# Chunks 0 to 3 of w_in: the low part from an fp32 product by the identity, and a new written order of the first phase

## The chip, the cores and the metric

One Trainium2 chip; the program runs on one of its cores. The time is device microseconds of one execution. The engines are TensorE (PE; PEld is its weight load), VectorE (DVE), ScalarE (ACT), GpSimd (POOL) and SyncE (SP), which issues nearly all DMAs here. Each engine takes its instructions strictly in the order in which the program gives them, and waits where an operand or a buffer is not ready.

## What is computed

Three layers in a row, for 4 batches of 576 tokens (heads of 64, model width 512):

```python
attn = softmax(q @ k.T / 8 - slope*|i-j|, over 128 keys back) @ v     # 8 heads, fp32
h = relu(x @ w_in); u, v = h[..., :512], h[..., 512:]                  # w_in: 512 x 1024
v_n = (v - mean(v)) / sqrt(var(v) + 1e-6)
gated = u * (w_spatial @ v_n + b_spatial)                              # 576 x 576
x = gated @ w_out                                                      # 512 x 512
out = sum over the best 2 of 4 experts of gate * (causal attention with wq, wk, wv) @ wo
```

w_in and w_out come as 64-bit floats, the rest as 32-bit floats. Products that need more than one pass are made from two parts of each factor, high and low, each rounded for TensorE's one-pass fp32 type (fp32r): high times high, high times low, low times high.

## The kernel before

The **first phase** covers the first attention and the spatial layer up to `gated`; the **second phase** folds w_out into the expert weights (`pw`, the product that opens it), projects (`pq`, `pvB`) and runs the causal attention. This change edits the first phase and a few lines at the start of the second.

In the first phase everything is cut into small steps with names, and three strings hold the order in which they are written: `OPENING`, `FIRST` and `SECOND` (lines 38 to 113). `step` (a nested function) turns a name into instructions. Within `OPENING` the order on every engine but the weights' own loads is exactly that of the string: an engine's program is the sequence of its own steps, so two steps that stand side by side but belong to different engines do not order one another. In `FIRST`, `SECOND` and the second phase only TensorE's order is written and a scheduler sets the others.

The steps that matter below. Tiles are numbered 0 to 19 in the order of the attention (batch 0: blocks 0, 1, 2, 3, 4 of 128 queries, the last of 64; batch 1 on: block 4 first).

- `raw n`, `q n`, `k n`, `v n`, `W n.ld`, `O n.ld`: loads on SP's queue. `raw` is a 128 x 512 chunk of w_in in 64-bit words; there are 8 chunks, 0 to 3 for the half of w_in that makes v, 4 to 7 for the half that makes u. Four buffers hold raw chunks and three hold q blocks, so a later load waits until an earlier chunk or block has been read.
- `C n.x`: chunk n is turned from 64-bit words into a high and a low part (lines 305 to 331). `abs` (ACT), `shl`, `or`, `mask`, `mul` (DVE, lines 379 to 382) give an fp32 value `w` and a remainder; `high` (ACT, line 320) rounds w; `rest` (DVE, line 207, called `lo_part`) subtracts the rounded value from w; `add` and `sec` (PE, lines 327 and 329) sum `rest` and the remainder in PSUM by products with an fp32r identity `one`; `low` (ACT, line 331) rounds the sum.
- `s i.g` (PE, lines 462 and 465): the scores of tile i for half g of the heads, fp32. `l i.g.*` (DVE, lines 480 and 229): mask and row minimum. `e i.g.*` (ACT, line 230): exponential and row sum. `f i.g.*` (DVE, lines 487 to 489): division by the sum. `t i.g` (PE, line 502): transposes. `c i.g` (ACT, line 504): eviction. `g i.g.*` (POOL): triangles. `a i` (PE, line 529): product with v. `xh i`, `xl i` (ACT line 541, DVE line 207): high and low part of the attention's output, which is the x of the next layer.
- `V b.t.n` (PE, line 555): a third of the product x times the v-half of w_in, for 128 tokens. `U b.s.m.n` (PE, line 618): a third of the u-half's. `P b.m.s.n` (PE, lines 633 and 636): a third of the spatial product; `pm` (DVE), `gs` (SP) gate and store it.
- `+n` behind a name: n fills, transposes of the identity into a PSUM bank that the step then overwrites (line 337). `warm` (line 344) issues 15 of them at the very start. They compute nothing.

One PSUM tile holds either a transposed tile or an attention product (`psT`, one buffer), two hold scores (`psS`), three hold the products of C, V, U and P (`psD`). So `t` and `a` follow each other through one buffer, with an eviction between any two.

At the start of the second phase, after the eight tiles of `pw`, `proj` of batch 0 runs while `gparts`, the copies of batch 1's gated values into `x2`, are spread between its parts.

Of the kernel before, what the change touches and what calls it, by code (L numbers as in the profile page):

```python
# [42 lines left out]
    t0.0 f1.0.rec C3.shl c0.0 l1.1.0 l1.1.1 l1.1.2 e1.1.0 a0 l1.1.3 e1.1.2 C3.or e1.1.1 q3 f1.0.mul s2.0 C3.high q4 C3.mask e1.1.3 l2.1.cp xh0 q5
    f1.1.add C3.rest l2.1.0 C3.add+8 l2.1.1 e2.1.0 l2.1.2 l2.1.3 e2.1.1 xl0 e2.1.2 f1.1.rec e2.1.3 C3.mul t1.0 f2.1.add C2.mul c1.0 C3.sec C3.low
    l2.0.cp g1.0.0 C2.sec raw6 C4.abs s3.0 f2.1.rec raw7 f1.1.mul C2.low W0.ld f2.1.mul C5.abs W1.ld t1.1 l2.0.0 g1.0.1 l2.0.1 V0.0.0 e2.0.0 l2.0.2
    l2.0.3 c1.1 C5.shl C4.shl e2.0.2 s3.1 C5.or e2.0.1 e2.0.3 C4.or t2.1 C5.high q6 f2.0.add g1.1.0 l3.0.cp C4.high V0.0.1 c2.1 f2.0.rec g1.1.1
    l3.1.cp V0.0.2 g2.1.0 W0.hi l3.0.0 l3.0.1 l3.0.2 e3.0.0 a1 g2.1.1 l3.0.3 l3.1.0 r0.0 l3.1.1 f2.0.mul W1.hi bn0.0 e3.1.1 e3.0.2 C4.mask s4.0 v7 xh1
    ag0.0 C5.mask C4.rest e3.1.0 e3.0.1 xl1 C4.add+4 e3.0.3 C5.mul t2.0 V0.1.0 f3.0.add C4.mul c2.0 l4.0.cp C6.abs g2.0.0 C4.sec f3.0.rec l3.1.2
    V0.1.1 l4.0.0 C4.low l4.0.1 g2.0.1 l3.1.3 e4.0.0 s4.1 C6.shl e4.0.1 f3.0.mul C7.abs a2 k10 f4.0.add e3.1.2 C6.or e3.1.3 q7 f4.0.rec C7.shl C6.high
    f3.1.add C6.mask s5.1 f3.1.rec f4.0.mul xh2 v8 f3.1.mul V0.1.2 xl2 C6.mul t3.1 r0.1 V0.2.0 C6.rest c3.1 bn0.1 g3.1.0 t3.0 C6.add ag0.1 C7.or c3.0  # L50
    C6.sec V0.2.1 C6.low l4.1.cp g3.1.1 l5.1.cp C7.high l4.1.0 g3.0.0 V0.2.2 l4.1.1 e4.1.0 l5.1.0 l5.1.1 g3.0.1 e4.1.1 t4.0 e5.1.0 s5.0 f4.1.add
    C7.mask c4.0 f4.1.rec e5.1.1 C5.rest a3 r0.2 q8 l5.0.cp g4.0.0 f5.1.add l5.0.0 g4.0.1 l5.0.1 e5.0.0 bn0.2 e5.0.1 s6.0 C7.rest xh3 v10 s6.1 ag0.2
    C7.mul n0.2.ln C7.add n0.2.ex q9 xl3 C7.sec C5.add O0.ld C7.low C5.sec f4.1.mul V0.3.0 f5.0.add O1.ld n0.2.r0 C5.low f5.1.rec f5.0.rec n0.2.r1
    f5.1.mul f5.0.mul t4.1 U0.1.1.0 W1.lo c4.1 U0.1.1.1 l6.0.0 g4.1.0 l6.0.1 t5.0 e6.0.0 l6.0.2 g4.1.1 U0.1.1.2 l6.0.3 e6.0.1 n0.2.r2 W0.lo U0.1.0.0
    c5.0 ur0.1.1 n0.2.r3 g5.0.0 a4 e6.0.3 W2.ld N0.0.sc O0.abs W3.ld N0.1.sc N0.0.hi s7.0 N0.2.sc v11 N0.1.hi N0.0.lo xh4 U0.1.0.1 N0.1.lo N0.2.hi
    V0.3.1 xl4 g5.0.1 e6.0.2 W2.hi N0.2.lo V0.3.2 W3.hi f6.0.add W2.lo t5.1 r0.3 U0.1.0.2 W3.lo W4.ld c5.1 U0.0.2.0 f6.0.rec ur0.1.0 bn0.3 W5.ld
    g5.1.0 U0.0.2.1 l6.1.0 g5.1.1 ag0.3 l6.1.1 U0.0.2.2 e6.1.0 l6.1.2 l6.1.3 e6.1.1 U0.0.3.0 l7.0.cp ur0.0.2 U0.0.0.0 e6.1.3 f6.0.mul e6.1.2 U0.0.0.1
    l7.0.0 W4.hi l7.0.1 t6.0 f6.1.add l7.0.2 e7.0.0 f6.1.rec U0.0.0.2 l7.0.3 W4.lo c6.0 U0.0.1.0 ur0.0.0 f6.1.mul U0.0.1.1 W5.hi O0.shl U0.0.1.2 O0.or
    t6.1 e7.0.1 U0.0.3.1 ur0.0.1 W5.lo c6.1 U0.0.3.2 O0.mask e7.0.2 a5 O0.mul e7.0.3 ur0.0.3 f7.0.add O0.add O2.ld s7.1 xh5 f7.0.rec f7.0.mul O0.hi
    s8.0 xl5 q10 O0.sh O0.lo a6 l7.1.cp O0.sl U0.1.2.0 l8.0.cp xh6 V0.4.0 l7.1.0 xl6 e7.1.0 l8.0.0 V0.4.1 l8.0.1 e8.0.0 l8.0.2 l8.0.3 e8.0.1 l7.1.1  # L60
    t7.0 l7.1.2 e8.0.2 l7.1.3 V1.0.0 e8.0.3 c7.0 f8.0.add f8.0.rec V1.0.1 e7.1.2 f8.0.mul e7.1.1 g7.0.0 e7.1.3 V1.0.2 O1.abs f7.1.add g7.0.1 f7.1.rec
    U0.1.2.1 r1.0 f7.1.mul U0.1.2.2 O1.shl t7.1 bn1.0 ur0.1.2 V0.4.2 c7.1 O1.or ag1.0 g7.1.0 t8.0 r0.4 U0.1.3.0 O1.mask c8.0 bn0.4 g7.1.1 U0.1.3.1
    U0.1.3.2 g8.0.0 ag0.4 n0.4.ln a7 O1.mul n0.4.ex ur0.1.3 n0.4.r0 g8.0.1 O3.ld n0.4.r1 n0.4.r2 n0.4.r3 O1.add s8.1 N0.3.sc xh7 v12 N0.4.sc N0.3.hi
    s9.1 xl7 q11 N0.4.hi l8.1.cp V1.1.0 N0.3.lo l8.1.0 V1.1.1 l8.1.1 l8.1.2 e8.1.0 l8.1.3 l9.1.cp e8.1.1 s9.0 e8.1.3 N0.4.lo e8.1.2 O1.hi V1.1.2 q12
    f8.1.add l9.1.0 O1.sh l9.1.1 e9.1.0 O1.lo P0.0.0.0 k15 e9.1.1 P0.0.0.1 l9.0.cp r1.1 O1.sl P0.0.0.2 l9.1.2 l9.0.0 e9.1.2 l9.1.3 l9.0.1 U1.0.0.0
    e9.0.0 l9.0.2 l9.0.3 e9.0.1 U1.0.0.1 pm0.0.0 e9.1.3 f8.1.rec bn1.1 U1.0.0.2 e9.0.3 P0.0.1.0 e9.0.2 f8.1.mul ur1.0.0 P0.0.1.1 f9.0.add f9.1.add
    ag1.1 f9.0.rec f9.1.rec t8.1 f9.0.mul P0.0.1.2 f9.1.mul c8.1 P0.1.0.0 g8.1.0 pm0.0.1 t9.1 gs0.0 g8.1.1 O2.abs P0.1.0.1 c9.1 P0.1.0.2 O2.shl O2.or
    U1.0.1.0 pm0.1.0 g9.1.0 U1.0.1.1 O2.mask U1.0.1.2 g9.1.1 a8 ur1.0.1 O2.mul O2.add O2.hi s10.1 v13 xh8 s10.0 O2.lo v14 P0.1.1.0 xl8 O2.sh q13
    l10.1.0 P0.1.1.1 l10.0.0 e10.1.0 l10.0.1 O2.sl P0.1.1.2 l10.0.2 e10.0.0 l10.0.3 l10.1.1 e10.0.2 l10.1.2 P0.2.0.0 l10.1.3 e10.0.1 pm0.1.1 P0.2.0.1
    e10.1.2 gs0.1 e10.0.3 P0.2.0.2 e10.1.3 f10.0.add e10.1.1 f10.0.rec U1.0.2.0 f10.0.mul P0.2.1.0 pm0.2.0 O3.abs P0.2.1.1 f10.1.add f10.1.rec  # L70
    f10.1.mul U1.0.2.1 O3.shl U1.0.2.2 O3.or P0.2.1.2 ur1.0.2 O3.mask P0.3.0.0 pm0.2.1 P0.3.0.1 O3.mul gs0.2 P0.3.0.2 O3.add U1.0.3.0 O3.hi pm0.3.0
    U1.0.3.1 O3.lo O3.sh U1.0.3.2 P0.3.1.0 O3.sl ur1.0.3 P0.3.1.1 P0.3.1.2 V1.2.0 pm0.3.1 gs0.3 t9.0 V1.2.1 c9.0 g9.0.0 t10.0 V1.2.2 c10.0 g9.0.1
    t10.1 r1.2 s11.1 c10.1 bn1.2 a9 ag1.2 l11.1.cp n1.2.ln n1.2.ex l11.1.0 n1.2.r0 l11.1.1 e11.1.0 l11.1.2 l11.1.3 e11.1.1 s11.0 n1.2.r1 v15 xh9
    n1.2.r2 n1.2.r3 N1.2.sc v16 e11.1.3 s12.0 xl9 e11.1.2 q14 N1.2.hi l11.0.cp a10 f11.1.add l12.0.cp U1.1.0.0 f11.1.rec xh10 l11.0.0 f11.1.mul
    U1.1.0.1 e11.0.0 l11.0.1 U1.1.1.0 l11.0.2 e11.0.1 l12.0.0 l11.0.3 U1.1.0.2 e11.0.2 l12.0.1 l12.0.2 e12.0.0 U1.1.2.0 l12.0.3 xl10 e12.0.2 U1.1.2.1
    e12.0.1 N1.2.lo U1.1.2.2 e12.0.3 ur1.1.0 N1.0.sc U1.1.1.1 e11.0.3 f12.0.add N1.1.sc U1.1.1.2 ur1.1.2 N1.0.hi f11.0.add f12.0.rec U1.1.3.0
    f11.0.rec f12.0.mul ur1.1.1 U1.1.3.1 N1.1.hi f11.0.mul U1.1.3.2 N1.0.lo t11.0 ur1.1.3 N1.1.lo V2.0.0 c11.0 g11.0.0 t11.1 V2.0.1 c11.1 g11.0.1
    g11.1.0 V2.0.2 g11.1.1 V1.3.0 r2.0 bn2.0 V1.3.1 ag2.0 V1.3.2 t12.0 r1.3 s12.1 c12.0 bn1.3 g12.0.0 a11 ag1.3 l12.1.cp q15 n1.3.ln g12.0.1 n1.3.ex
    l12.1.0 n1.3.r0 l12.1.1 e12.1.0 n1.3.r1 l12.1.2 e12.1.1 n1.3.r2 s13.1 l12.1.3 v17 n1.3.r3 xh11 N1.3.sc e12.1.2 xl11 s13.0 e12.1.3 N1.3.hi l13.1.cp
    V2.1.0 l13.0.cp q16 l13.1.0 l13.0.0 V2.1.1 e13.1.0 l13.0.1 l13.0.2 e13.0.0 l13.0.3 l13.1.1 e13.0.2 V2.1.2 l13.1.2 l13.1.3 e13.0.3 f12.1.add  # L80
    N1.3.lo e13.1.2 s14.0 r2.1 f12.1.rec f12.1.mul e13.1.3 s14.1 e13.1.1 bn2.1 t12.1 e13.0.1 q17 f13.1.add ag2.1 f13.1.rec P1.0.0.0 f13.0.add
    f13.1.mul c12.1 P1.0.0.1 l14.1.cp g12.1.0 f13.0.rec P1.0.0.2 l14.1.0 l14.1.1 e14.1.0 g12.1.1 P1.0.1.0 e14.1.1 pm1.0.0 P1.0.1.1 f13.0.mul t13.1
# [1119 lines left out]
```

## Time and profile before

| | us |
|---|---|
| median of 3 runs | 478.71 (478.48 to 478.85) |
| the profiled execution | 478.61 |
| its span in the trace | 476.9 |
| PE busy | 464.6 (97%) |
| PEld busy | 412.4 (86%) |
| DVE busy | 303.6 (64%) |
| ACT busy | 266.2 (56%) |

The span runs from the first instruction to the last; 1.7 us of the execution's time lie outside it. Busy shares are means over the whole span: the opening looks quite different from the rest. PE's records overlap by a part of their length, so PE's busy time overstates what it costs to run a row of matmuls; where the chain of work that ended last passes through PE, its pieces show the spacing instead. [...]

### The profile page before, as it was taken

To read this page: it belongs to the slowest core of one execution; us is meant where nothing else is said; L and a number is where in the kernel's file an instruction comes from. 1 tells how busy PE (TensorE), PEld (TensorE's weight loads), DVE (VectorE), ACT (ScalarE), POOL (GpSimd) and SP (SyncE) were. 2 spreads that over 40 slices of the span, in tenths; PEclk is the share of its full clock that TensorE was granted. 3 is DMA by queue.
4 is the path that set the end of the run, shared out by engine and by line. 5 is a ranking of instruction groups with operands and counts; after the bars stand their busy time and mean duration, and the time that the engine had idled before them with its cause. 6 is when DMAs were issued, how large, how long until landed. Compare 5 with 4: busy or idle time off the path is not lost.

```text
span 476.9 us, 10486 instructions
## 1 busy us (share of the span) xinstructions
PE 464.6 (97%) x3867; PEld 412.4 (86%) x3867; DVE 303.6 (64%) x1100; ACT 266.2 (56%) x793; POOL 94.2 (20%) x208
## 2 busy tenths in 40 slices
...
GB/s 259 377 263 93 182 168 180 89 191 150 96 52 67 92 52 49 0 1 26 51 290 107 160 60 100 1 101 0 2 23 3 1 45 1 1 1 68 90 89 88
DMA packets 22518, 43.75 MB, mean 92 GB/s; under 512 B 3522, under 2 KB 5954, under 8 KB 22084
## 3 DMA queue, kind: packets, MB, share of 16 engines
...
## 4 chain that ended last, share of the span: by engine, by line
PE 94%; DVE 3%; DMA 2%; ACT 1%; issue 0%; POOL 0%; POOLq 0%; ACTq 0%; DVEq 0%
PE pu L618 11%; PE pv L555 11%; PE pg L633 11%; PE pq L909 10%; PE px L529 7%; PE pvB L871 6%; PE pxB L1025 6%; PE ps L462 5%; PE pout L1060 5%; PE ptB L1004 5%; PE psB L958 4%; PE pw L774 4%; PE pt L502 3%; PE pg L636 2%; DMA q<-in_qP 2%; PE psB L960 1%
## 5 line engine op out<-in xcount | busy, mean ns | idle before, releaser
L230 ACT ACTIVATE p<-p,st 128x128 f32<-128x128 f32 x144 | 56.4, 394 | 11.6 <-DVE st L229 11.2
L909 PE MATMUL pq<-x,W 128*128 128x288 f32 x384 | 58.5, 302 | 0.8 <-DVE k L207 0.8
L555 PE MATMUL pv<-win,x 128*128 128x512 f32 x216 | 57.8, 407 | 0.0
L633 PE MATMUL pg<-wsp,vn 128*128 128x288 f32 x384 | 57.7, 297 | 0.0
L511 POOL TENSOR_SCALAR_AFFINE_SELECT pU<-pT 128x512 f32<-128x512 f32 (+1 forms) x32 | 20.0, 624 | 183.9 <-ACT pT L504 181.7
L618 PE MATMUL pu<-x,win 128*128 128x288 f32 x384 | 56.1, 298 | 0.0
L909 PEld LDWEIGHTS pq<-x,W 128*128 128x128 f32 x384 | 52.0, 188 | 3.7 <-issue 1.7
L633 PEld LDWEIGHTS pg<-wsp,vn 128*128 128x128 f32 x384 | 52.9, 188 | 0.6 <-issue 0.2
L618 PEld LDWEIGHTS pu<-x,win 128*128 128x128 f32 x384 | 52.2, 188 | 1.1 <-issue 0.7
L242 POOL TENSOR_SCALAR pB<-pB,stB 128x384 f32<-128x384 f32 (+4 forms) x64 | 35.7, 575 | 69.6 <-DVE stB L981 58.3
L555 PEld LDWEIGHTS pv<-win,x 128*128 128x128 f32 x216 | 39.1, 191 | 8.6 <-issue 1.0
L230 ACT ACTIVATE pB<-pB,stB 128x128 f32<-128x128 f32 (+3 forms) x64 | 35.6, 558 | 14.7 <-DVE stB L229 14.7
L504 ACT COPY pT<-pt 128x512 f32<-128x512 f32 (+1 forms) x40 | 21.6, 540 | 29.1 <-PE pt L502 28.9
L462 PE MATMUL ps<-k,q 64*128 64x256 f32 (+1 forms) x256 | 31.2, 378 | 3.1 <-DMA q<-in_qP 2.0
L229 DVE CUSTOM_DVE_ANT_0 pB<-psB,trit 128x128 f32<-128x128 f32 (+3 forms) x64 | 28.2, 486 | 9.2 <-PE psB L958 8.9
L229 DVE CUSTOM_DVE_ANT_0 p<-ps,relm 128x128 f32<-128x128 f32 x128 | 29.7, 282 | 4.1 <-PE pt L502 2.5
L1004 PE MATMUL ptB<-ident,pB 128*128 128x128 f32 (+1 forms) x200 | 30.3, 274 | 0.3 <-DVE pTB L1005 0.3
L641 DVE TENSOR_TENSOR g<-u,pg 128x288 f32<-128x288 f32 x32 | 14.3, 452 | 24.8 <-PE pg L636 23.2
L462 PEld LDWEIGHTS ps<-k,q 64*128 64x128 f32 x256 | 21.8, 193 | 9.2 <-issue 3.2
L1060 PE MATMUL pout<-wo,o 128*128 128x512 f32 x102 | 29.6, 412 | 0.0
L1025 PE MATMUL pxB<-pTB,vt 128*64 128x128 f32 (+2 forms) x480 | 28.3, 262 | 0.0
L1025 PEld LDWEIGHTS pxB<-pTB,vt 128*64 128x64 f32 (+1 forms) x480 | 23.1, 136 | 5.6 <-issue 3.4
...
## 6 DMA issues: line engine op xcount, KB each, us to landing
...
gf<-g_dram SPq DMA_DIRECT2D x4, 1152.0 KB, 5.6
raw<-in_w_in SPq DMA_DIRECT2D x8, 512.0 KB, 6.9
...
k<-in_kP SPq DMA_DIRECT2D x3, 1152.0 KB, 7.0
rawo<-in_w_outT SPq DMA_DIRECT2D x4, 512.0 KB, 5.1
```

What stands on the lines that cost most here:

```text
L229: lambda: nc.vector.tensor_tensor_reduce(s_view, ps_view, tab, -0.125, FLT_MAX, ALU.add, ALU.min, nm),
L230: lambda: nc.scalar.activation(s_view, s_view, AF.Exp, bias=nm, scale=-1.0, accum_out=sm),
L242: nc.gpsimd.tensor_scalar(p, p, r, 0.0, op0=ALU.mult, op1=ALU.add)
L462: nc.tensor.matmul(ps[:, o, 256 * h : 256 * h + kn], Q_[b, j][r, hp, :], K_[b][r, hp, k0 : k0 + kn], start=True, stop=True)
L529: nc.tensor.matmul(px[64 * o : 64 * o + 64, hp, :qn], V_[b, t][:, h * 64 : h * 64 + 64], rhs, start=(t == max(0, j - 1)), stop=(t == j))
L555: nc.tensor.matmul(pv, x[i][:, k, t0 : t0 + P], win[j][:, k, 512:1024], start=(n == 0 and k == 0), stop=(n == 2 and k == 3))
L618: nc.tensor.matmul(pu[:, :HALF], win[i][:, k, m * P : (m + 1) * P], x[j][:, k, c], start=(n == 0 and k == 0), stop=(n == 2 and k == 3))
L633: nc.tensor.matmul(pg[:, :HALF], vn[i][k][:, m * P : (m + 1) * P], wsp[j][:, k, c], start=(n == 0 and k == 0), stop=False)
L909: nc.tensor.matmul(pq[:, :HALF], W[i][:, k, c0 : c0 + P], G[j][:, k, c], start=(n == 0), stop=(n == 11))
L1004: nc.tensor.transpose(pt[:kb, n, :], p[pr][:, o, c0 : c0 + kb], ident)
L1025: nc.tensor.matmul(px[64 * o : 64 * o + 64, pr, :qn], vt[:kb, c, (2 * pr + o) * 64 : (2 * pr + o) * 64 + 64], rhs, start=(c == 0), stop=(c ...
L1060: nc.tensor.matmul(po[:tn], o2[i][:, pr, :tn], wos[j][:, pr, :], start=(n == 0), stop=(n == 5))
```

## The change

For chunks 0 to 3 of w_in the step `rest` is gone. TensorE takes w itself in full fp32 by the fp32 identity (`sum`), subtracts the rounded value by a second fp32r product with minus the identity (`minus`), and adds the remainder as before (`sec`). Chunks 4 to 7 keep `rest`, `add` and `sec`. One ACT instruction at the start makes the negative identity. The three strings are new: the same steps otherwise, in another order on every engine and on SP's queue; of the 50 fills (23, 15, 8 and 4) 6 are left, ahead of the first scores. The first strip of the second phase issues the copies into `x2` ahead of `proj` instead of between its parts.

```diff
 OPENING = """
-    raw0 q0 k0 raw1 raw2 k2 k1 q1 T1 T0 C0.abs q2 C0.shl C0.or C0.mask C0.high v0 C0.mul C0.rest C0.add+23 C0.sec k3 s0.1 C0.low s0.0 l0.1.0 l0.1.1
...
+    T1 raw0 q0 k0 raw1 C0.abs q1 k1 s0.1+6 s0.0 k2 raw2 q2 raw3 q3 C0.shl C0.or C0.mask C0.mul C0.high T0 l0.1.0 l0.1.1 l0.1.2 l0.1.3 C0.sum C0.minus
...
     one = const.tile([P, P], F32R, name="one")
+    minus = const.tile([P, P], F32R, name="minus")
     nc.scalar.copy(one, ident)
+    nc.scalar.mul(minus, ident, -1.0)
...
-        elif name == "add":
+        elif name in ("add", "sum"):
             live[n].append(psD.tile([P, 512], F32, tag="D", name=f"psw{n}"))
-            fill(live[n][4][:, :P])
-            nc.tensor.matmul(live[n][4], one, live[n][3], start=True, stop=False)
+            fill(live[n][-1][:, :P])
+            first = (ident, live[n][1]) if name == "sum" else (one, live[n][3])
+            nc.tensor.matmul(live[n][-1], *first, start=True, stop=False)
+        elif name == "minus":
+            nc.tensor.matmul(live[n][-1], minus, hi, start=False, stop=False)
         elif name == "sec":
-            nc.tensor.matmul(live[n][4], one, lo, start=False, stop=True)
+            nc.tensor.matmul(live[n][-1], one, lo, start=False, stop=True)
...
     G, gparts = load_g(1, gfp)
-    dense.pull(3000.0)
     for _ in gparts:
-        dense.pull(1500.0)
+        pass
     dense.drain()
```

SP's queue, loads 4 to 15 of the program before (`raw` a chunk of w_in, `q`, `k`, `v` blocks of the attention's inputs; the trailing number is a buffer's):

```order
L298 DMA raw_184<-in_w_in 128x512
L298 DMA raw_186<-in_w_in 128x512
L437 DMA k_182<-in_kP 128x4x128 x2
L432 DMA q_1_190<-in_qP 128x512
L432 DMA q_2_194<-in_qP 128x512
L445 DMA v_0_200<-in_v 128x512
L437 DMA k_182<-in_kP 128x4x128
L298 DMA raw_248<-in_w_in 128x512
L298 DMA raw_261<-in_w_in 128x512
L660 DMA reltail<-in_relt 128x512
L437 DMA k_182<-in_kP 128x4x64
L439 DMA k_295<-in_kP 128x2304
```

The block q 3 stands only 9 loads behind this piece, after 3 loads of v, raw 5 and 4 more of v. The same place now:

```order
L300 DMA raw_186<-in_w_in 128x512
L437 DMA q_1_190<-in_qP 128x512
L442 DMA k_184<-in_kP 128x4x128 x2
L300 DMA raw_210<-in_w_in 128x512
L437 DMA q_2_212<-in_qP 128x512
L300 DMA raw_214<-in_w_in 128x512
L437 DMA q_3_216<-in_qP 128x512
L450 DMA v_0_281<-in_v 128x512
L450 DMA v_1_283<-in_v 128x512
L300 DMA raw_285<-in_w_in 128x512
L437 DMA q_4_287<-in_qP 128x512
L442 DMA k_184<-in_kP 128x4x128
```

q 3 has moved to the tenth place of the queue, and the whole K of batch 1 (128x2304) from the fifteenth to the twenty-fifth.

PE, the last rows before the first product with w_in (`pv`, step V 0.0.0) in the program before (`ps` scores, `pt` transposes, `psw` the sums of the chunks):

```order
L462 MATMUL ps_2_0_394<-k_182,q_2_194 128x256 x4
L337 MATMUL psw_413<-ident 128x128 x8
L327 MATMUL psw_413<-vn_3_115,one 128x512
L502 MATMUL pt_1_0_433<-ident,p_1_0_312 128x128 x4
L329 MATMUL psw_413<-win_99,one 128x512
L329 MATMUL psw_357<-win_99,one 128x512
L462 MATMUL ps_3_0_454<-k_182,q_3_391 128x256 x4
L502 MATMUL pt_1_1_475<-ident,p_1_1_362 128x128 x4
L555 MATMUL pv_0_485<-win_98,x_102 128x512 x4
```

And now:

```order
L330 MATMUL psw_367<-u_108,ident 128x512
L332 MATMUL psw_367<-win_100,minus 128x512
L467 MATMUL ps_3_1_370<-k_184,q_3_216 128x256 x4
L334 MATMUL psw_367<-win_101,one 128x512
L330 MATMUL psw_376<-u_109,ident 128x512
L507 MATMUL pt_1_0_393<-ident,p_1_0_263 128x128 x4
L332 MATMUL psw_376<-win_100,minus 128x512
L334 MATMUL psw_376<-win_101,one 128x512
L507 MATMUL pt_1_1_404<-ident,p_1_1_315 128x128 x4
L560 MATMUL pv_0_411<-win_100,x_104 128x512 x4
```

The fills are gone, each chunk has three products instead of two, and the scores of tile 3 that need q 3 stand some way ahead of the first `pv` instead of just before it.

## Rows read from the trace of the kernel before

**Rows 1.** Stretches: us; busy (instructions) of PE, PEld, DVE, ACT, POOL; clock; DMA share; GB/s
```profile
5.76:32.11 26.35, 20.04 (x138) 14.49 (x137) 24.76 (x92) 17.85 (x59) 3.55 (x6) 0.92 1.05 350
32.11:35.50 3.39, 3.39 (x15) 2.10 (x13) 0.98 (x4) 2.78 (x9) 1.27 (x2) 0.61 0.33 128
5.76:76.85 71.09, 64.53 (x526) 52.25 (x524) 65.56 (x236) 54.95 (x171) 14.95 (x25) 0.95 0.68 223
110.00:271.90 161.90, 161.90 (x1321) 148.29 (x1320) 98.17 (x341) 78.40 (x248) 21.39 (x40) 1.00 0.25 85
```
**Rows 2.** Timeline of PE: start, us, instruction, [idle before, releaser]
```profile
29.34 2.08 PE L462 MATMUL ps<-k,q 64*128 64x256 f32 x8 [2.04 <-DMA q<-in_qP]
32.11 2.05 PE L555 MATMUL pv<-win,x 128*128 128x512 f32 x4
76.98 0.77 PE L529 MATMUL px<-pT,v 128*64 128x128 f32 x10
271.92 1.39 PE L774 MATMUL pw<-wc,wt 128*128 128x386 f32 x7
294.62 1.58 PE L909 MATMUL pq<-x,W 128*128 128x288 f32 x10 [0.76 <-DVE k L207]
```
**Rows 3.** Chain of work that ended last, pieces on PE: start, us of the piece
```profile
49.76 0.46 PE pt L502 x4
50.22 0.23 PE psw L327
50.45 0.23 PE psw L329
52.74 0.65 PE ps L465 x4
53.46 1.97 PE px L529 x32
55.43 1.09 PE ps L462 x16
57.65 0.93 PE pv L555 x4
58.79 1.06 PE pu L618 x8
61.14 1.08 PE px L529 x32
62.22 1.06 PE ps L462 x8
```
**Rows 4.** Groups of instructions on DVE, 0 to 110 us: shapes, count, busy us, mean ns
```profile
L229 DVE CUSTOM_DVE_ANT_0 p<-ps,relm 128x128 f32<-128x128 f32 x68 | 15.7, 280 | 1.5 <-PE ps L462 1.5
...
L207 DVE TENSOR_TENSOR vn<-u,win 128x512 fp32r<-128x512 f32 x8 | 5.4, 679 | 0.0
...
L207 DVE TENSOR_TENSOR wsp<-st_wsp,wsp 128x576 fp32r<-128x576 f32 x4 | 2.9, 745 | 0.0
```
**Rows 5.** Timeline of DVE: the first chunk's first step, and the low part of tile 5
```profile
5.76 0.43 DVE L379 TENSOR_SCALAR u<-f 128x512 int32<-128x512 int32 x1 [2.02 <-ACT f L378]
10.19 0.29 DVE L229 CUSTOM_DVE_ANT_0 p<-ps,relm 128x128 f32<-128x128 f32 x1 [1.48 <-PE ps L462]
76.17 0.68 DVE L207 TENSOR_TENSOR x<-px,x 128x512 fp32r<-128x512 f32 x1
```
**Rows 6.** DMA issues by line: count, KB each, median us from issue to landing
```profile
raw<-in_w_in SPq DMA_DIRECT2D x8, 512.0 KB, 6.9
k<-in_kP SPq DMA_DIRECT2D x3, 1152.0 KB, 7.0
```
**Rows 7.** Timeline of PE in the first 9 us: warm-up transposes and fills
```profile
1.42 3.46 PE L344 MATMUL warm<-ident 128*128 128x128 f32 x15 [1.42 <-POOL ident masks.py:199]
6.81 1.37 PE L337 MATMUL psw<-ident 128*128 128x128 f32 x8
```
**Rows 8.** Busy time by stretch around the wait for q 3
```profile
28.00:30.00 2.00, 0.66 (x4) 0.57 (x6) 2.00 (x11) 1.33 (x4) 1.79 (x4) 0.50 1.05 398
```

More of the change, by code (lines that the diff above doesn't have):

```diff
@@ L43 @@
[L43 to L82, printed above, removed]
@@ new lines @@
+    C0.sec s1.0 l0.0.0 l0.0.1 l0.0.2 e0.1.0 C1.abs e0.1.3 e0.1.2 e0.1.1 C1.shl l0.0.3 C1.or f0.1.add C1.mask s1.1 e0.0.0 e0.0.1 f0.1.rec C1.mul
+    l1.0.cp f0.1.mul l1.0.0 l1.0.1 l1.0.2 l1.0.3 C0.low e0.0.2 e0.0.3 C2.abs C1.high f0.0.add e1.0.1 C3.abs v0 v1 raw4 q4 k3 reltail v2 k4 raw5 C1.sum
+    t0.1 C1.minus s2.1 C1.sec c0.1 e1.0.0 e1.0.2 e1.0.3 l1.1.cp C2.shl l1.1.0 f0.0.rec l1.1.1 f0.0.mul l1.1.2 l1.1.3 t0.0 s2.0 C2.or l2.1.cp C3.shl
+    l2.1.0 l2.1.1 f1.0.add C2.mask l2.1.2 l2.1.3 C3.or C2.mul f1.0.rec C3.mask e1.1.0 c0.0 C1.low e1.1.3 e1.1.1 C2.high e1.1.2 a0 C2.sum C2.minus s3.1
@@ new lines @@
+    C2.sec C3.sum e2.1.3 e2.1.2 xh0 C4.abs C3.high f1.1.add f1.0.mul xl0 f1.1.rec C3.mul f1.1.mul e2.1.0 e2.1.1 C2.low t1.0 c1.0 C3.minus C3.sec
+    C3.low t1.1 V0.0.0 V0.0.1 V0.0.2 C5.abs c1.1 g1.0.0 g1.0.1 g1.1.0 g1.1.1 l2.0.cp f2.1.add l2.0.0 l2.0.1 l2.0.2 l2.0.3 f2.1.rec C5.shl e2.0.3
+    e2.0.2 e2.0.1 e2.0.0 f2.1.mul l3.1.cp t2.1 l3.1.0 f2.0.add l3.1.1 f2.0.rec l3.1.2 f2.0.mul l3.1.3 s3.0 r0.0 c2.1 t2.0 c2.0 e3.1.3 e3.1.2 s4.1
+    g2.1.0 g2.1.1 g2.0.0 g2.0.1 a1 C5.or l3.0.cp l3.0.0 l4.1.cp l3.0.1 e3.1.1 e3.1.0 l3.0.2 l3.0.3 e3.0.3 xh1 e3.0.0 e3.0.1 l4.1.0 l4.1.1 C4.shl C4.or
@@ new lines @@
+    xl1 e3.0.2 f3.1.add f3.1.rec f3.1.mul C5.mask f3.0.add C5.mul C4.mask C4.mul f3.0.rec C5.high raw6 v3 v4 raw7 W0.ld k5 e4.1.0 e4.1.1 s4.0 q5 q6
+    W1.ld W1.hi q7 s5.0 a2 xh2 W0.hi V0.1.0 V0.1.1 V0.1.2 C6.abs C7.abs C4.high xl2 f4.1.add f4.1.rec C5.rest f4.1.mul C6.shl C7.shl f3.0.mul t3.1
+    C5.add C5.sec c3.1 V0.2.0 t3.0 V0.2.1 V0.2.2 g3.1.0 g3.1.1 l4.0.cp C7.or l4.0.0 l4.0.1 c3.0 g3.0.0 g3.0.1 C7.mask C6.or l5.0.cp t4.1 C7.high r0.1
+    C5.low c4.1 s5.1 l5.0.0 l5.0.1 C4.rest l5.1.cp C6.mask l5.1.0 C7.mul l5.1.1 C7.rest e5.0.0 a3 s6.1 s6.0 C4.add C7.add C7.sec C4.sec e5.0.1 xh3
@@ new lines @@
+    r0.2 xl3 e4.0.0 e4.0.1 C6.high e5.1.0 C6.mul f4.0.add f5.0.add f4.0.rec f4.0.mul f5.0.rec C6.rest C4.low V0.3.0 t4.0 V0.3.1 C6.add C6.sec V0.3.2
+    C7.low c4.0 e5.1.1 C6.low bn0.1 f5.0.mul W0.lo W1.lo l6.0.0 l6.0.1 l6.0.2 t5.0 l6.1.0 l6.1.1 l6.0.3 bn0.2 l6.1.2 r0.3 e6.0.2 c5.0 bn0.0 f5.1.add
+    O0.ld q8 q9 O1.ld W2.ld W3.ld U0.1.0.0 U0.1.0.1 U0.1.1.0 U0.1.1.1 U0.1.1.2 U0.1.0.2 O0.abs e6.0.1 e6.0.0 e6.1.0 ur0.1.1 e6.0.3 g4.0.0 g4.1.0
+    g4.1.1 g5.0.0 g5.0.1 g4.0.1 U0.1.3.0 a4 xh4 e6.1.2 e6.1.1 ur0.1.0 l6.1.3 e6.1.3 f5.1.rec O0.shl O0.or O0.mask f6.0.add O0.mul f5.1.mul xl4
```

86 lines of the change are left out of this document (55 added, 31 removed).

## The prediction

> **What bounds the kernel now.** I read the time by stretch first. From 110 to 271.9 us PE is busy for all of 161.9 us at the full clock [rows 1]; after that its timeline shows one gap, 0.76 us before a `pq` at 294.62 [rows 2]. So from about 35 us on nothing but PE's own work counts, and the time is that work plus what PE lost before. The opening is another stage: between 5.76 and 32.11 us DVE is busy for 24.76 of 26.35 us, PE for 20.04, and the DMA engines are full (share 1.05, 350 GB/s) [rows 1]. DVE, which turns w_in into two parts, all but sets the opening, and the loads come next.
>
> The timeline of PE then shows where q 3 landed: its scores start at 29.34 after an idle 2.04 us, the first `pv` (V 0.0.0) not before 32.11 [rows 2]. [...]
>
> To put a number on the loss I use the **lateness** of a step: its start, less all PE work written ahead of it. The prices are pieces of the chain of waits, where records don't overlap [rows 3]: four transposes or fills 0.46, so 0.11 each; a product of 512 columns in the one-pass type 0.23; a third of V 0.93, of U 0.53; a half's scores 1.06 (0.55 in the first block, 0.65 in the last); an attention product 1.97 (1.08 for 64 queries). Ahead of V 0.0.0 stand 16.1 us of work: it is 16.0 late. Ahead of tile 5's two-part product with v (the piece of ten that starts near 76.98 [rows 2] is its neighbour, and holds the start, about 77.06) stand 58.4 us: 11.2 V, 9.5 U, 14.2 scores, 5.3 transposes, 9.0 attention, 3.7 for the 16 products that split w_in, 5.5 for 50 fills. It is 18.7 late. At the fold (271.92 [rows 2], 252.2 of work ahead) it is 19.7. All that this change can gain is in these 19 us, or in the work itself.
>
> **The change, part by part.**
>
> *Work on PE.* 44 fills go: 44 x 0.11 = -4.84. `minus` takes the place of `add` at the same 0.23: nothing. Four `sum` are added, fp32 with 512 columns. No such product is in the trace; the nearest is the scores of the last block, 0.65 for four records that are two products of 192 columns [rows 3], so 1.69 ns a column and 0.87 for 512. [...] I take 0.87, the row of the real product: +3.48. Sum -1.4.
>
> *Work on DVE.* Four `rest` go, 0.68 each [rows 4]: -2.7. The new order also carries steps over this place. I compare up to the same step, the low part of tile 5 (76.17, done 76.85 [rows 5]). Behind it go three low parts of v_n, one row statistic and two low parts of the spatial weights (0.68 and 0.75 a piece [rows 4]) with three small ones: -4.7. Ahead of it come half a softmax (four row pieces of 0.28 [rows 4] with their readouts, a mask, two small ones) and five passes over a chunk of w_out: +5.5. The 65.6 us of DVE work in 5.76 to 76.85 [rows 1] become 63.7.
>
> *Loads.* Ahead of q 3 stood 8064 KB, now 3584. It landed at 29.34; by its share of the bytes it lands near 13 to 14, long before its scores are written. The 2.04 us hole goes, and with it DVE's idle 2.4 us behind it (3.39 less 0.98 [rows 1]). What is late next in the opening is the first softmax: DVE sat 1.48 us ahead of 10.19 until the scores came [rows 5]; I leave that in.
>
> *The opening, then.* DVE starts at 5.76 on the first chunk [rows 5]. Up to the low part of chunk 3 the new order has 18.1 us of its work; with 1.5 idle and 0.44 for eviction, V 0.0.0 starts near 25.8, with 15.2 us of PE work ahead: 10.6 late instead of 16.0. PE could not catch up by more, as its products follow DVE's parts.
>
> *The attention of batch 0.* With 63.7 us of DVE work and the old idle 5.5 (71.09 less 65.56 [rows 1]) less the hole's 2.4, the low part of that tile is done at 5.76 + 63.7 + 3.1 = 72.6. PE has 61.3 us ahead of the product behind it (six U thirds and one half's scores more than before, four sums, six fills): 11.3 late, 7.4 less than before. From there on PE was never kept waiting before, and in the new order no producer stands nearer to its consumer on PE.
>
> *The fold and the drain.* ACT's four copies into `x2` stand right behind the same eviction in both orders, and PE's order there is unchanged. I cost this at nothing: behind it lies the pull of the weight products, and the 0.76 us gap at 294.62 [rows 2] stays, some 9 us earlier. If that cover fails, the same gap grows by at most one eviction of four, under 2 us. The negative identity, 0.3 us of ACT while it waits for the first load, is hidden.
>
> **Sum:** -1.4 of work and -7.4 of lateness, -8.8. Against the profiled execution's 478.61 (span 476.9) that is 469.8; the median of the runs shown is 478.71, 0.1 above it, so **469.9**.
>
> *Bounds.* With no idle DVE the lateness is 10.2 for V 0.0.0's chain: 468.7. Sums at 0.44 take 1.7 more: 467.0. With all the old idle of 5.5 on DVE the lateness is 13.7: 472.2. [...]
>
> [...] The fills are what kept PE busy. [...] The gap of 2.04 us was followed by 0.50 [rows 8]. [...]
>
> **The rivals.**
>
> 1. *The clock stays low in the opening (slower).* After the warm-up transposes end at 4.9 us PE has only six fills and then scores that wait for q 0, k 0 and the first chunk; nothing fills the waits for DVE. In its place: everything up to V 0.0.0. [...] 478.6 - 1.4 + 3.7 = **480.9**. It decides from a lateness of 20.1, that is 8.7 us lost to the clock, some 17 us at the lower level on the path. For it: 0.50 after a gap of only 2.04 us [rows 8]. Against it: DVE is the slower engine in this stage, so PE at half speed has slack to lose first; and PE's 15 us of work in 20 are not far from its old share.
>
> 2. *A late load takes the place of q 3.* The new queue puts the K of batch 1 (1152 KB, 7.0 us from issue to landing [rows 6]) ahead of the v block that tile 5's product in the new order needs, and the queue stands behind a load that waits for DVE's low part of a w_out chunk: 53.4 us of DVE work, near 62.1. The K goes out then, the v block lands near 69.5, and PE arrives at 58.1 + 11.3 = 69.4. There is no margin: 2 to 3 us lost once would give **472.5**. For: eight chunks of 512 KB took 6.9 us each to land in a full queue [rows 6]. Against: at 60 us the queue is no longer full (0.68 over the whole stretch against 1.05 in the opening [rows 1]).
>
> 3. *Only the work counts.* The lateness is made again somewhere in FIRST by DVE, whose 65.56 of 71.09 us [rows 1] leave it little slack, and only the 1.4 of work and one or two us stay: about **476**. For: DVE loses only 1.9 us of work up to the place compared. Against: the hole of 2.04 us and the idle of DVE behind it are gone for a reason that the queue shows.
>
> 4. *The change does nothing for the time.* It would need the lateness to come out at 20, rival 1 at half strength: within 1 us of 478.7.
>
> **How the numbers follow.** The forecast with its bounds (467.0 to 474.5, rival 2 within it) has 0.78, rival 3 (474.5 to 477.7) 0.09, rival 4 0.03, rival 1 0.10. About 0.2%, 1 us, is what a measurement of this kernel can tell from no change. So faster 0.87, same 0.03, slower 0.10. The range 467.0 to 474.5 leaves out rivals 1, 3 and 4, 0.22 together, so I stretch it to 475.0, which takes in a little of rival 3.
>
> **What the profile of the changed kernel would show.** Right: the scores of tile 3 start without a wait for q 3, which lands before 15 us; V 0.0.0 starts at 25 to 27; DVE has no gap over 1.5 us from 8 to 35 us; `sum` rows of 0.87 us; the first `pw` near 263; the 0.76 us gap near 286. Wrong: a granted clock near 0.5 over most of 7 to 25 us, with V 0.0.0 past 30 (rival 1); PE idle near 70 us, released by a load of v (rival 2); V 0.0.0 on time but the fold at 270 (rival 3). If `sum` takes over 1.2 us the product is not what I priced; if the `pq` gap grows, the drain is not free.

## The result, and the profile after

The changed kernel takes 474.15 us (median of 4 runs, 473.99 to 474.43) against 478.6 us beside it: ratio 0.991, 95% interval 0.9893 to 0.9927. It is faster by 4.5 us, about half of the 8.8 that the prediction gave. The time lies inside the range; the forecast itself was almost twice too large.

PE's timeline of the changed kernel, at the places of [rows 2] and at the longest of its waits from there on (start us, us, engine, line, operation, tiles; in brackets the idle time before and what ended it):

```profile
24.07 3.01 PE L560 MATMUL pv<-win,x 128*128 128x512 f32 x12
...
29.51 0.63 PE L507 MATMUL pt<-ident,p 128*128 128x128 f32 x4 [0.52 <-DVE p L494]
...
35.27 0.44 PE L534 MATMUL px<-pU,v 128*64 128x128 f32 x4 [0.90 <-DVE st L492]
...
71.08 0.34 PE L534 MATMUL px<-pU,v 128*64 128x64 f32 x4 [0.96 <-DMA v<-in_v]
...
74.47 0.66 PE L507 MATMUL pt<-ident,p 128*128 128x128 f32 x4 [0.16 <-DVE x L209]
...
245.56 6.67 PE L623 MATMUL pu<-x,win 128*128 128x288 f32 x48 [1.03 <-ACT u L626]
...
266.94 17.19 PE L779 MATMUL pw<-wc,wt 128*128 128x386 f32 x96
285.30 12.94 PE L914 MATMUL pq<-x,W 128*128 128x288 f32 x96 [1.17 <-DVE W L209]
```

The wait for q 3 is gone, and V 0.0.0 starts at 24.07 instead of 32.11. The fold, the clearest mark of what the first phase cost, starts 4.98 us earlier than in [rows 2]. The rest of the program got 0.5 us longer, nearly all of it in the wait ahead of the first `pq`. Behind 40 us three waits are new: 0.96 us for a load of v, 1.03 us for an eviction of u, and 1.17 us where 0.76 stood before.

Busy time by stretch, to set beside [rows 1] (us; busy us and instructions of PE, PEld, DVE, ACT, POOL; clock; DMA share; GB/s):

```profile
5.76:24.07 18.31, 16.34 (x106) 10.10 (x105) 18.21 (x74) 16.17 (x57) 0.33 (x1) 1.00 1.01 338
24.07:37.16 13.09, 11.35 (x107) 9.06 (x105) 12.81 (x49) 10.08 (x37) 8.27 (x12) 1.00 0.72 253
28.00:30.00 2.00, 1.48 (x13) 1.06 (x14) 2.00 (x12) 0.58 (x1) 1.27 (x2) 1.00 1.03 424
```

VectorE is busy for 18.21 of the 18.31 us up to V 0.0.0: it all but sets that stage. The granted clock, given as a share of its full speed, reads 1.00 in all three stretches, with six fills; the 0.50 of [rows 8] is gone. (The trace's record of the clock begins at 7.08 us here and at 7.48 before; the 1.00 ahead of that is a blank, not a reading.)

The lateness of the prediction (a step's start less the PE work ahead of it, by the same prices) shows where the gain went (us):

| step | before | after | gained in lateness |
|---|---|---|---|
| V 0.0.0 | 32.11 - 16.1 = 16.0 | 24.07 - 15.2 = 8.9 | 7.1 |
| behind tile 5's product | 18.5 to 18.7 | 74.47 - 61.3 = 13.2 | 5.4 |
| u product at 245.56 (after) | 19.7 | 14.8, then 16.1 behind its wait | 4.9, then 3.6 |
| fold | 271.92 - 252.2 = 19.7 | 266.94 - 250.8 = 16.1 | 3.6 |

The 3.6 and the 1.4 of work saved are the 5.0 at the fold.

### The profile page after: what moved, and what is told of

The parts are those of the page before. It is cut to its first block, busy times and chain, and to the rows that moved or that the text cites. A ratio compares the mean times of both kernels' runs of the same rounds, so it can differ in the third digit from the quotient of the medians.

```text
span 472.4 us, 10405 instructions
## 1 busy us (share of the span) xinstructions
PE 460.4 (97%) x3831; PEld 407.7 (86%) x3831; DVE 302.2 (64%) x1096; ACT 263.5 (56%) x794; POOL 97.0 (21%) x208
## 4 chain that ended last, share of the span: by engine, by line
PE 85%; DMA 4%; ACT 3%; DVE 3%; SPq 2%; issue 1%; ACTq 0%; DVEq 0%
PE pq L914 11%; PE pg L638 10%; PE pv L560 9%; PE pu L623 8%; PE px L534 6%; PE pvB L876 6%; PE pxB L1030 6%; PE pout L1065 5%; PE ptB L1009 5%; PE psB L963 4%; PE ps L467 4%; PE pw L779 4%; PE pt L507 3%; DMA raw<-in_w_in 2%; PE pg L641 2%; DMA st_wsp<-in_wspT 2%
## 5 line engine op out<-in xcount | busy, mean ns | idle before, releaser
L638 PE MATMUL pg<-wsp,vn 128*128 128x288 f32 x384 | 58.7, 297 | 0.0
L516 POOL TENSOR_SCALAR_AFFINE_SELECT pU<-pT 128x512 f32<-128x512 f32 (+1 forms) x32 | 21.8, 688 | 167.4 <-ACT pT L509 167.1
L560 PE MATMUL pv<-win,x 128*128 128x512 f32 x216 | 55.1, 399 | 0.0
L232 ACT ACTIVATE pB<-pB,stB 128x128 f32<-128x128 f32 (+3 forms) x64 | 35.6, 559 | 14.8 <-DVE stB L231 14.8
L231 DVE CUSTOM_DVE_ANT_0 p<-ps,relm 128x128 f32<-128x128 f32 x128 | 31.3, 284 | 6.3 <-PE ps L467 3.0
L232 ACT ACTIVATION_READ_ACCUMULATOR p<-p,st 128x1 f32 x144 | 27.4, 190 | 0.0
```

The source lines that it names most:

```text
L231: lambda: nc.vector.tensor_tensor_reduce(s_view, ps_view, tab, -0.125, FLT_MAX, ALU.add, ALU.min, nm),
L232: lambda: nc.scalar.activation(s_view, s_view, AF.Exp, bias=nm, scale=-1.0, accum_out=sm),
L560: nc.tensor.matmul(pv, x[i][:, k, t0 : t0 + P], win[j][:, k, 512:1024], start=(n == 0 and k == 0), stop=(n == 2 and k == 3))
L638: nc.tensor.matmul(pg[:, :HALF], vn[i][k][:, m * P : (m + 1) * P], wsp[j][:, k, c], start=(n == 0 and k == 0), stop=False)
```

## Experiments

Times are medians beside runs of the kernel before on the same chip. The start of the fold in the profile (271.92 before, 266.94 after) is given too; it shows the first phase alone, but of one execution. From the fold to the end it is 205.0 to 205.5 us in every trace, so the several microseconds by which some kernels' runs spread must lie mostly ahead of that mark, and it has to be read beside the median. Two traces whose first phase is the same program (the changed kernel and the one with the old drain, below) differ there by 0.63 us.

### One part of the change at a time

**The sums alone.** In the old strings of the kernel before:

```diff
-C0.rest C0.add+23
+C0.sum+23 C0.minus
...
```

and so for chunks 1 to 3, with `sum`, `minus` and the negative identity as in the change.

> The kernel before with sum and minus for chunks 0 to 3, in the old order and with all fills. Theory A: V 0.0.0 still waits for q 3, which lands at 29.3 us, so the four sums lie in waiting time and VectorE's 2.7 us are not what is waited for: 478 to 479 us, no change. Theory B: 475 to 476.5 us.

Measured: 478.29 us, ratio 1.0001 (0.9987 to 1.0015); fold at 271.12. PE's wait for q 3 is what it was:

```profile
29.21 1.13 PE L467 MATMUL ps<-k,q 64*128 64x256 f32 x8 [2.17 <-DMA q<-in_qP]
```

The sums by themselves bring nothing measurable; theory A. The 0.8 us at the fold are no gain of theirs. In this trace the clock fell later and for a shorter time behind the same wait; in the kernel before it is 0.50 from 28.0 us on [rows 8]:

```profile
28.00:30.00 2.00, 0.79 (x8) 0.69 (x8) 2.00 (x11) 1.08 (x4) 1.78 (x4) 1.00 1.06 406
30.00:32.00 2.00, 2.00 (x11) 1.53 (x8) 1.93 (x3) 0.82 (x3) 0.62 (x2) 0.65 1.02 390
32.00:34.00 2.00, 2.00 (x8) 1.18 (x9) 0.92 (x3) 1.96 (x8) 1.11 (x2) 0.50 0.49 189
```

The mean granted clock sorts the 58 runs of the kernel before that stand beside the experiments: at 0.993 (36 runs, as in its profile) they take 478.4 to 479.5 us, at 0.996 (21) 477.2 to 478.3, at 1.000 (one) 476.23. The profiled run with the sums is one at 0.996, and its 477.92 us lie within what the kernel before takes at that clock.

**The early q 3 alone.** The kernel before, one load moved in the string:

```diff
-... raw3 ... q3 ...
+... raw3 q3 ...
```

> The kernel before with the load of q 3 moved up in the queue, behind raw 3, and nothing else. Theory A: the idle 2.04 us and the stretch at the lower clock behind it go, V 0.0.0 near 29.5 to 30.5: 475 to 476.5 us, half or more of the whole gain. Rival (VectorE is right behind q 3 as the bound): V 0.0.0 near 31.5 and 477.5 to 478.6 us.

Measured: 476.29 us (476.22 to 476.3), ratio 0.995 (0.9935 to 0.9965); V 0.0.0 at 28.72, fold at 269.50. One moved load gives 2.4 of the 4.5 us. V 0.0.0 came earlier than expected. The mean clock of these four runs is 0.996 to 1.000, and they take what the one run of the kernel before at 1.000 took (476.23). How much of the 2.4 us is the wait itself, and how much the lower clock behind it, was not separated.

**Both, in the old order.**

> The kernel before with the early q 3 and with sum and minus for chunks 0 to 3, in the old order and with all fills. Theory A (with q 3 out of the way VectorE's pace sets the opening, and the sums take 2.7 us from it): lateness falls from the 17.3 at the fold of the early q 3 alone to 13 or 14 while the work rises by 3.5: 475.5 to 477 us, about the early q 3 alone (476.3) or a little less. Theory D (the sums only pay where the order is made for them): 477.5 us or more.

Measured: 476.53 us, ratio 0.9972 (0.9952 to 0.9991); V 0.0.0 at 28.32, fold at 269.72. That is inside theory A's range. **And without fills:**

> The same without the 50 fills. Theory A (the three products per chunk keep the clock up, the fills are work on TensorE's path where q 3 no longer makes it wait): 472 to 474.5 us, near the changed kernel without its order, granted clock 0.95 or more from 6 to 30 us. Theory D: 475.5 us or more, the rest being the order's.

Measured: 477.55 us, ratio 0.9982 (0.9972 to 0.9992); V 0.0.0 at 28.77, fold at 269.50, in the shortest of its ten runs (476.24). Here theory A falls, in its time and its clock (0.91 below): with q 3 early, VectorE's four passes gone and 5.5 us of fills gone from PE, V 0.0.0 starts where q 3 alone had put it. The stretch from 5.76 to 24 us tells why. First the early q 3 alone, then with the sums and without fills, each with VectorE's longest wait in it:

```profile
5.76:24.00 18.24, 14.21 (x119) 10.70 (x117) 16.64 (x64) 13.01 (x44) 0.00 (x0) 1.00 1.04 365
```
```profile
10.20 0.29 DVE L229 CUSTOM_DVE_ANT_0 p<-ps,relm 128x128 f32<-128x128 f32 x1 [1.48 <-PE ps L462]
```
```profile
5.76:24.00 18.24, 13.76 (x86) 9.11 (x86) 14.66 (x60) 13.08 (x44) 0.00 (x0) 0.91 1.04 366
```
```profile
10.48 0.29 DVE L231 CUSTOM_DVE_ANT_0 p<-ps,relm 128x128 f32<-128x128 f32 x1 [2.41 <-PE ps L467]
```

VectorE's busy time falls by 2 us, and VectorE idles for them, about half of it ahead of the first scores: in the old order its steps stand behind others that aren't ready. Its work isn't what sets V 0.0.0 there.

**The new order alone.** The changed kernel, with the old way to the low part:

```diff
-C0.sum ... C0.minus
+... C0.rest C0.add
...
```

> The changed kernel with the old way to make the low parts of chunks 0 to 3 (VectorE's rest and the one-pass add in place of sum and minus), in the new order of everything else. Theory A (the new order with the early q 3 brings the gain, the sums trade TensorE work for VectorE work): four products of 0.87 us go from TensorE, four passes of 0.68 come to VectorE, which sets the lateness up to the attention of batch 0; lateness grows by up to 2.7 and the work falls by 3.5, so 473 to 474.5 us, the same as the changed kernel or a little faster. Theory B (the sums are what shortens the opening): VectorE is late by 2.7 and more, 476 us or above.

Measured: 477.43 us (475.62 to 479.0), ratio 0.9969 (0.9952 to 0.9986); V 0.0.0 at 28.17, fold at 270.24. Theory A falls here too, and B's time holds. PE's timeline, at three of the four `add`, and a stretch behind the first of them:

```profile
9.61 0.52 PE L330 MATMUL psw<-vn,one 128*128 128x512 f32 x1 [1.79 <-DVE vn L209]
...
15.55 0.50 PE L330 MATMUL psw<-vn,one 128*128 128x512 f32 x1 [0.80 <-DVE vn L209]
...
23.06 0.50 PE L330 MATMUL psw<-vn,one 128*128 128x512 f32 x1 [2.60 <-DVE vn L209]
```
```profile
10.00:15.00 5.00, 4.52 (x22) 2.90 (x20) 4.84 (x22) 4.26 (x18) 0.00 (x0) 0.66 1.04 393
```

PE waits 5.2 us for the results of `rest`, the clock falls to 0.66 behind the first of these waits, and VectorE is as busy as in the changed kernel (17.97 of 18.24 us up to 24 us) but has 2.7 us more to do. V 0.0.0 comes 4.1 us later. What each of these costs isn't separated: every `rest` stands right ahead of its `add` in this string, another place for it was not tried, and part of the 4.1 us can be the clock.

So the parts don't add up: by the ratios, q 3 alone gives 0.5%, the sums alone nothing, q 3 and the sums 0.3%, the new order without the sums 0.3%, and all together 0.9%. At the fold of one execution each that is 2.4, 0.8 (the clock's, see above), 2.2, 1.7 and 5.0 us. The new order keeps VectorE fed (18.14 of 18.24 us up to 24 us), and only there do the sums count.

### The fills and the clock

> The kernel before without its 50 fills. Theory A: TensorE waits for q 3 anyway, the fills lie in waiting time: 478 to 479 us, granted clock near 0.9 or more up to 28 us, V 0.0.0 near 32. Theory C (the fills hold the clock up): a granted clock near 0.5 over much of 7 to 28 us, V 0.0.0 past 33, 479.5 us or above.

```diff
-... C0.add+23 ... s1.0+15 ... C3.add+8 ... C4.add+4 ...
+... C0.add ... s1.0 ... C3.add ... C4.add ...
```

The kernel before with these fills taken out: 479.06 us, ratio 1.0009 (0.9996 to 1.0022); V 0.0.0 at 30.63, fold at 271.37. Its stretch from 20 to 25 us:

```profile
20.00:25.00 5.00, 4.08 (x26) 2.84 (x24) 4.46 (x17) 3.49 (x13) 0.00 (x0) 0.50 1.04 339
```

The clock does fall: 0.50 here, 0.77 on the mean of 5.76 to 24 us. Yet the time is the same to what can be told: theory A has the time right and the clock wrong, theory C the other way round. V 0.0.0 even comes 1.5 us earlier than with the fills. The slower PE still fits into what the opening leaves it.

> The changed kernel with 46 of the fills back, at the places that they had (23 ahead of the first chunk's sum, 15 ahead of the scores of tile 1, 8 ahead of the last sum). Theory A (the three products per chunk keep TensorE busy, its clock was 1.00 throughout, VectorE sets the pace up to the second tile's product): the fills fall partly into idle time; of their 5.1 us between 1 and 4 come on top, 475 to 478 us, granted clock unchanged. Theory C (the fills buy clock): 473.5 us or less.

```diff
-... C0.sum ... s1.0 ... C3.sum ...
+... C0.sum+23 ... s1.0+15 ... C3.sum+8 ...
```

The changed kernel with them back: 477.54 us (475.6 to 479.63), ratio 0.9985 (0.9963 to 1.0006), its median 3.4 us above the changed kernel's; fold at 271.12, 4.2 us later, in a run of 478.49. No fall of the clock is on record, as without them: it is 1.00 from 10 to 50 us. The first scores, before any of these fills, are slower in this trace; first the changed kernel, then this one:

```profile
6.63 1.36 PE L467 MATMUL ps<-k,q 64*128 64x128 f32 x16 [0.47 <-DMA k<-in_kP]
```
```profile
6.70 2.08 PE L467 MATMUL ps<-k,q 64*128 64x128 f32 x16 [0.54 <-DMA k<-in_kP]
```

So of 46 x 0.11 = 5.1 us, between 3 and 4 land on the path. In the changed kernel fills would be pure cost. With the sums and six fills the clock over 5.76 to 24 us is 1.00; in the same order with `rest` in their place, and the same six fills, it is 0.90.

### The three new waits

**The load of v at 71.08.** SP's queue in the changed kernel:

```profile
61.78 0.33 SPq L418 DMA_DIRECT2D wt_dram<-hio  x1
62.51 0.33 SPq L419 DMA_DIRECT2D wt_dram<-loo  x1
62.88 0.45 SPq L444 DMA_DIRECT2D k<-in_kP  x1
63.37 0.45 SPq L450 DMA_DIRECT2D v<-in_v  x1
```

The K goes out at 62.88, as rival 2 had worked out (near 62.1); it is the third batch's, not the second's as the prediction has it. PE stands ready for tile 5 at 70.12 (predicted 69.4) and waits 0.96 us. In the string:

```diff
-k10 v5 ... v6 v7 v8 ...
+v5 ... v6 v7 v8 k10 ...
```

> The changed kernel with the load of the third batch's K (k 10, 1152 KB) moved behind the loads v 5 to v 8. If that load made the wait of 0.96 us ahead of tile 5's product at 71.08, the wait goes, the lateness there is 11.9 instead of 13.0, and 0.9 to 1.4 us are gained: 472.8 to 473.3. Rival (VectorE is right behind, at the low part of that tile): the product behind it waits instead and less than 0.4 us is gained.

Measured: 474.61 us (472.93 to 478.74), ratio 0.9936 (0.9906 to 0.9967); fold at 266.94, exactly as in the changed kernel. The wait at tile 5 is gone (its product starts at 70.07), and another takes its place five microseconds on. PE, then ACT, whose eviction PE waits for:

```profile
73.08 0.66 PE L507 MATMUL pt<-ident,p 128*128 128x128 f32 x4
...
76.44 0.66 PE L507 MATMUL pt<-ident,p 128*128 128x128 f32 x4 [1.78 <-ACT pT L509]
```
```profile
74.42 0.67 ACT L370 CAST wsp<-st_bias 32x576 fp32r<-32x576 f32 x1 [2.25 <-DMA st_bias<-in_bsp]
75.11 0.67 ACT L371 CAST bias_hi<-st_bias 1x576 fp32r<-1x576 f32 x1
75.80 0.58 ACT L509 COPY pT<-pt 128x512 f32<-128x512 f32 x1
```

The bias rows are the next loads of the same queue behind the K, and their casts stand ahead of the eviction on ACT. The rival of this run had the right effect (nothing gained) with another engine as its cause.

**The eviction of u at 245.56.** ACT and SP of the changed kernel:

```profile
240.33 1.65 ACT L595 CAST vn<-vr 128x512 fp32r<-128x512 f32 x3
244.37 0.83 ACT L212 CAST wc<-st_wc 128x772 fp32r<-128x772 f32 x1 [2.39 <-issue]
245.11 0.40 ACT L626 ACTIVATE u<-pu 128x288 f32<-128x288 f32 x1
```
```profile
234.09 3.74 SPq L762 DMA_DIRECT2D wt<-wt_dram  x8
237.93 0.45 SPq L768 DMA_DIRECT2D st_wc<-in_wcat  x1
238.47 0.38 SPq L715 DMA_DIRECT2D g_dram<-g  x1
239.30 0.33 SPq L768 DMA_DIRECT2D st_wc<-in_wcat  x1
```

ACT idles 2.39 us ahead of a cast of an expert weight whose load went out behind eight others; the evictions of u, already due, stand behind that cast, and PE waits for them to free a `psD` buffer. (The row names no releaser for the 2.39 us; that it is the load is what the edit tests.) The edit:

```diff
-        st = d2.tile([P, NW], F32, tag="f64w", name=f"st_wc{k}", bufs=2)
+        st = (d2 if k < 2 else fp).tile([P, NW], F32, tag="f64w", name=f"st_wc{k}", bufs=2)
...
-    later = deque([load_wcat(0), load_wcat(1)])
+    later = deque([load_wcat(k) for k in range(4)])
```

with the eight loads of `wt` behind these.

> The changed kernel with all four staging loads of the expert weights (wcat) issued ahead of the eight loads of the folded w_out parts, two of them into buffers of their own. If ScalarE's cast of the third and fourth, which waits 2.39 us for its load and stands ahead of the evictions of u, makes the idle 1.03 us of TensorE at 245.56, that gap goes and 0.9 to 1.5 us are gained: 472.7 to 473.3. Rival (the gap comes from the order of the u products and their evictions): the gap stays, 474.2.

Measured: 472.9 us (472.58 to 473.37), ratio 0.9888 (0.9867 to 0.991); the gap is gone, the fold starts at 265.79, 1.15 us earlier, and the median is 1.25 us below the changed kernel's.

**The first pq.** After the change the first `pq` waits for VectorE's last low part of the fold; before, it started at once and the fourth waited. The built programs are read as putting the first `pq` into the PSUM bank of the fold's eighth product after the change and not before; no row here shows the banks. The wait goes with the written order: it is 1.17 us, ahead of the first `pq`, in the new order with the old `rest` too, and 0.76 us, ahead of a later one, in the old order with the sums. Is it the moved copies into `x2`? The changed kernel with the old lines there:

```diff
+    dense.pull(3000.0)
     for _ in gparts:
-        pass
+        dense.pull(1500.0)
```

> The changed kernel with the old start of the second phase: the copies into x2 between the parts of proj again. If these lines cost and bring nothing: 474 to 474.5 us, and still 1.1 to 1.2 us of wait ahead of the first pq, because the buffer that the first pq takes is the one of the last product of the fold in both. Rival (the x2 copies ahead of proj made the wait): the wait is 0.76 us, ahead of a later pq, and 0.4 us are gained.

Measured: 474.39 us (473.44 to 474.45), ratio 0.9919 (0.9904 to 0.9934); the wait is 1.16 us, still ahead of the first `pq`. The edit of the second phase is worth nothing either way. Now both of the loads' edits above, and a turn of the buffers:

```diff
+    nc.vector.memset(psD.tile([P, 512], F32, tag="D", name="turn")[:, :1], 0.0)
     dense.add(proj(0, G), 18000.0)
```

> The changed kernel with both of these edits, and with a tile of the projection's three PSUM buffers taken and cleared by VectorE before the projection starts, so that its first product does not land in the buffer of the last product of the fold. If the three waits are separate: the 1.17 us ahead of the first pq becomes 0.76 us ahead of the fourth, and the time is 1.0 + 1.2 + 0.4 below the changed kernel, 471.2 to 472.0. Rival (they cover each other): 472.7 or more.

Measured: 473.05 us (471.13 to 474.51), ratio 0.9888 (0.9849 to 0.9928); fold at 264.37. The same kernel once more:

> The kernel with the K load behind v, the early loads of the expert weights and the turned PSUM buffers once more, beside the others on the same chip: 471 to 472.5 us; its profiled span was 469.4 us against the changed kernel's 472.4.

Measured: 472.33 us (471.09 to 474.12), ratio 0.9884 (0.9855 to 0.9912); fold at 264.65. PE, in the first of the two:

```profile
264.37 10.80 PE L776 MATMUL pw<-wc,wt 128*128 128x386 f32 x60
...
287.11 8.20 PE L913 MATMUL pq<-x,W 128*128 128x288 f32 x60 [0.80 <-DVE k L209]
```

The wait is 0.80 us ahead of a later `pq`, as it was before the change: the turned buffer does it. The eviction behind tile 5 still holds PE up, 0.36 us in this trace and 1.05 in the second:

```profile
75.13 0.66 PE L507 MATMUL pt<-ident,p 128*128 128x128 f32 x4 [1.05 <-ACT pT L509]
```

The profiled spans are 469.4 and 469.7 us against 472.4, some 3 us shorter. But these are two of the shorter runs: four of the eight take 471.1 to 471.7 us, the other four 473.2 to 474.5, and of those there is no trace. The medians are 1.1 and 1.8 us below the changed kernel's; they are the lowest here together with that of the early weight loads, from which the ratios can't tell them. By its median of 473.05 the first of the two lies with its rival; that the K's place and the turn add anything to the early weight loads is not shown.

## Why the prediction was half right

- **Work on PE**: held. A `sum` takes 0.86 us by its neighbours (21.47 to 22.33 below), as priced from the last block's scores. `minus` was put at the 0.23 of `add`; the spacing behind it is 0.31 (22.69 to 23.00), so the work saved was overstated by a few tenths in all. The lower bound of 467.0 puts a `sum` at 0.44; no run shows that term, only the 0.86.

```profile
21.47 1.02 PE L330 MATMUL psw<-u,ident 128*128 128x512 f32 x2
22.33 0.60 PE L507 MATMUL pt<-ident,p 128*128 128x128 f32 x4
22.69 0.48 PE L332 MATMUL psw<-win,minus 128*128 128x512 f32 x1
23.00 0.39 PE L334 MATMUL psw<-win,one 128*128 128x512 f32 x1
```

- **The opening**: the mechanism held, and it was better than forecast: V 0.0.0 at 24.07, not 25.8, mainly because VectorE lost 0.1 us instead of 1.5. (The 10.2 of the lower bound doesn't come out of the prediction's own terms: without the 1.5 of idle they give 9.1 for V 0.0.0, close to the 8.9 measured.) It then gave back most of that to tile 2, where the lateness is 35.27 - 23.8 = 11.5, in the place of the 11.3 that the prediction had for tile 5. What it said of the parts was incomplete: costed one by one against VectorE's total, they looked as if they added up, and the runs show that they don't.

- **The step that failed** is "From there on PE was never kept waiting before, and in the new order no producer stands nearer to its consumer on PE", together with "the 0.76 us gap ... stays". So the term of -7.4 us of lateness measured -3.6 at the fold. The distance between producer and consumer was counted for engines only. The late things of the changed kernel behind 40 us are a load, a cast that waits for a load and holds up the evictions behind it on ACT, and one PSUM buffer. The missing 4.3 us are 2.0 around tile 5 (5.4 gained there instead of 7.4), 0.5 in small drifts up to 245 us, 1.3 at 245.56, and 0.5 at the first `pq` and behind it. Of the 2.0, 1.4 hang on the load of v: with the K behind it the transposes behind tile 5's product start at 73.08 instead of 74.47. That the 1.3 hang on the weights' loads is shown by 1.25 us at the median without that wait. The rest is read from the traces. With the three waits moved or shortened the shorter runs take 471.1 us, 1.2 from the forecast; the medians, 473.05 and 472.33, are 3.2 and 2.4 from it, and that part stays open.

- **Rival 2** came true in its place, at 0.96 us instead of 2 to 3. It should have been in the forecast rather than beside it, since the text itself found no margin, and the loads queued behind had to be in the price, too. The K that it names is the third batch's. Its time, 472.5, was still 1.6 below what was measured.

- **Rival 1**, the slower one, fell: the granted clock of the changed kernel is 1.00 from where its record begins, at 7.08 us, to 471 us. The fills do go with the clock in the old order: over 5.76 to 24 us it is 0.77 without them and 1.00 with them. In the changed kernel, with six fills and with the products of the sums, it is 1.00. The step from the clock to the time depends on the place. That old kernel without fills was no slower (ratio 1.0009). But the kernel before, whose profile has 0.50 from 27.96 us, inside the wait for q 3, to 34.79, takes 478.4 to 479.5 us in its runs at a mean clock of 0.993 and 477.2 to 478.3 at 0.996 (which of the two brings the other was not tested). No run shows the 3.7 us of lateness that this rival adds, nor the 2.3 us between 472.2 and the range's upper bound of 474.5, which were for an opening at a lower clock. In their place V 0.0.0 came 7.1 us less late, at a clock of 1.00.

- **Rival 3** (476: only the work counts) was too low a gain, by 1.8 us. **Rival 4** (no change) fell: the interval of the ratio ends at 0.9927.
